# First loads of a four-layer transformer kernel moved between two DMA queues, and eight idle matmuls in place of ten

## The chip, the cores and the metric

The kernel runs on one core of a Trainium2 chip. The metric is the time of one execution on the device in microseconds (us); lower is better. Before the change it was 1632.44 us (median of three, 1632.38 to 1632.49).

## The reference

Two linear-attention layers (A) and two gated feed-forward layers (B) alternate on x of 2048 x 1024 in bf16. Only the start of the first layer A matters here: a layer norm of x, then the projection onto K.

```python
def _layernorm(x, axis=-1, eps=1e-5):
    m = jnp.mean(x, axis=axis, keepdims=True)
    v = jnp.var(x, axis=axis, keepdims=True)
    return (x - m) / jnp.sqrt(v + eps)
...
    x = x + _A_ref(_layernorm(x, axis=-1), A_wqkv, A_wo)   # q, k, v = x @ wqkv, ...
    x = x + _B_ref(_layernorm(x, axis=-1), B_W_gate, B_W_up, B_W_down)
    # and both once more
```

## The kernel before

The head loads x in blocks of 128 rows (256 KB; `load_x(t, c)` takes half c of block t) and the K weights k0 (in two halves of 512 KB) and k1 (1 MB). Everything without a queue goes to SyncE's queue. At the start of an execution TensorE's clock is slow: in the profile before, its matmuls start 0.43 us apart until 8.1 us and 0.22 us apart afterwards. So the head gives it matmuls on zeros ("idle" matmuls) while the first data come.

```python
def head(self):
    zero = self.ep.tile([P, NW], BF16, tag="e")
    nc.vector.memset(zero, 0.0)                      # after VectorE's other constants
    idle = self.ps3.tile([P, NW], F32, tag="b")
    for _ in range(10):
        nc.tensor.matmul(idle, lhsT=zero[:, 0:P], rhs=zero, start=True, stop=True)

    k0, k1, v0, q0, q1 = (ring.place() for _ in range(5))
    self.load_x(0, 0, nc.scalar)
    self.load_x(0, 1)
    self.load_x(1, None, nc.scalar)
    k0(0, H)
    self.load_x(2, None, nc.scalar)
    k0(H, 2 * H)
    self.load_x(3, None, nc.scalar)
    k1()
    q0()
    self.load_x(4)
    ...
```

The order of work for the first two blocks, which VectorE and ScalarE keep as written. Note `stat(1, 0)`, which stands before the scaling of block 0:

```python
def block0():
    stat(0, 0); stat(0, 1); rstd(0)      # VectorE, VectorE, ScalarE
    stat(1, 0)                           # first half of block 1
    scale(0, 0); scale(0, 1)             # VectorE
    t0 = turn(0, 0); t1 = turn(0, 1)     # TensorE: 4 transposes each
    t0("s"); stat(1, 1); rstd(1); t1("v")
    k(0, 0, between)                     # 8 matmuls; 1 to 4 read the first half of k0
```

`between` scales and transposes half of block 1 ahead of the last two of the eight. Then follow K unit (1,0) (block 1, k0), K unit (0,1) (block 0, k1), and so on.

## Time and profile before

| | |
|---|---|
| time, executions of the kernel before (31 timed in all, in four calls) | medians 1632.47 to 1632.53, all 1632.25 to 1633.73 us |
| the execution that was profiled | 1632.99 us, span 1631.2 us |

TensorE's busy time and its waits stand in the prediction below.

The timeline of VectorE in the profile before (start in us, duration in us, engine, line, operation, tiles; in brackets the idle time and what ended it):

```profile
3.61 1.29 DVE L142 BATCH_NORM_STATS2 st<-x 128x6 f32<-128x512 bf16 x2 [1.57 <-DMA x<-in_A_x_dram]
4.93 0.21 DVE L147 BATCH_NORM_AGGREGATE mv<-st 128x2 f32<-128x12 f32 x1
5.14 0.69 DVE L142 BATCH_NORM_STATS2 st<-x 128x6 f32<-128x512 bf16 x1
5.75 0.72 DVE L158 TENSOR_SCALAR x<-x,mv,rstd 128x512 bf16<-128x512 bf16 x2
```

TensorE's timeline in slices of 0.1 us shows where its clock became full (xN: so many in the slice, the first at the time in front):

```profile
8.06 0.62 PE L403 MATMUL ps<-t,xnT 128*128 128x512 bf16 x2
8.30 0.59 PE L403 MATMUL ps<-t,xnT 128*128 128x512 bf16 x2
8.52 0.38 PE L403 MATMUL ps<-t,xnT 128*128 128x512 bf16 x1
```

From 8.06 on the starts are 0.24 and 0.22 us apart, where they were 0.43 before.

### The profile page before, as it was taken

Reading aid. Unit: us, or ns where it says so; the run is one execution under the profiler, and the core shown is the slowest. Engines: PE = TensorE matmul, PEld = TensorE weight load, DVE = VectorE, ACT = ScalarE, POOL = GpSimd, SP = SyncE. Lnnn points to the kernel's source line nnn. Section 1 sums busy time; section 2 is a strip of 40 time slices with the busy share of each in tenths; the row PEclk is TensorE's granted clock in tenths of the full one; section 3 lists DMA queues with packets and bytes.
Section 4 is the critical chain, followed back from the end, with each engine's and each line's share of the span. In section 5 each row is a group of like instructions: output and inputs, shape, how many; then the busy total and the mean of one; then the engine's idle time right before and its main releaser. Section 6 shows DMA issues by size and latency. Waiting matters only on the chain.

```text
span 1631.2 us, 18462 instructions
## 1 busy us (share of the span) xinstructions
PE 1625.2 (100%) x7658; PEld 743.1 (46%) x7658; DVE 570.8 (35%) x947; ACT 331.2 (20%) x636; POOL 201.5 (12%) x134
## 2 busy tenths in 40 slices
PE   9999999999999999999999999999999999999999
PEld 4444444444444444444444444444444444444444
DVE  7855695113212222222264547941022111211211
ACT  6741212101110110111066312121011101101110
POOL 2349220000000000000023592100000000000000
PEclk9999999999999999999999999999999999999999
DMA  8313637448445445544550147464554454454452
GB/s 248 62 52 59 175 71 201 145 151 232 155 145 188 160 150 162 168 151 138 166 124 1 52 98 244 84 193 145 179 166 149 156 186 155 145 165 155 155 161 72
DMA packets 298245, 235.05 MB, mean 144 GB/s; under 512 B 101296, under 2 KB 294192, under 8 KB 298160
## 3 DMA queue, kind: packets, MB, share of 16 engines
q1 hardware_dynamic: 292832, 228.75, 47.5%
q10 hardware_dynamic: 5328, 5.11, 0.9%
q8 instruction: 60, 0.98, 0.2%
q14 instruction: 25, 0.20, 0.0%
HBM read 201.33 MB, written 8.39 MB: 129 GB/s over the span
## 4 chain that ended last, share of the span: by engine, by line
PE 98%; ACT 1%; DMA 0%; DVE 0%; issue 0%; SPq 0%
PE pu L628 24%; PE pg L628 24%; PE acc L652 23%; PE ps L403 12%; PE ps L520 7%; PE ps L437 7%; DMA t<-in_A_wqkv_dram 0%; PE kv L450 0%; PE fold L508 0%; PE acc_last L652 0%; ACT e L355 0%; ACT e L354 0%; ACT e L356 0%; PE tp L264 0%; DVE pq L362 0%
## 5 line engine op out<-in xcount | busy, mean ns | idle before, releaser
L628 PEld LDWEIGHTS <-t 128*128 128x128 bf16 x3584 | 350.7, 98 | 422.8
L628 PE MATMUL pu<-xnT,t 128*128 128x512 bf16 x1792 | 423.3, 379 | 0.0
L628 PE MATMUL pg<-xnT,t 128*128 128x512 bf16 x1792 | 423.3, 379 | 0.0
L652 PE MATMUL acc<-t,hT 128*128 128x512 bf16 x1764 | 382.5, 379 | 0.0
L634 DVE TENSOR_TENSOR hT<-pu,rg 128x512 bf16<-128x512 f32 x224 | 154.6, 690 | 572.9 <-PE pu L628 572.9
L633 ACT ACTIVATE rg<-pg 128x512 f32<-128x512 f32 x224 | 133.5, 596 | 737.4 <-PE pg L628 737.4
L652 PEld LDWEIGHTS <-hT 128*128 128x128 bf16 x1820 | 178.1, 98 | 209.0
L403 PE MATMUL ps<-t,xnT 128*128 128x512 bf16 x1024 | 224.7, 379 | 1.0 <-DMA t<-in_A_wqkv_dram 0.6
L403 PEld LDWEIGHTS <-xnT 128*128 128x128 bf16 x1024 | 99.8, 98 | 121.2 <-issue 1.8
L520 PE MATMUL ps<-T,pqT 128*128 128x512 bf16 x512 | 111.8, 379 | 0.0
L149 ACT ACTIVATE rstd<-mv,eps 128x1 f32<-128x1 f32 x64 | 18.7, 293 | 327.8 <-DVE mv L147 327.7
L669 DVE TENSOR_TENSOR xo<-x,acc 128x512 bf16<-128x512 f32 x31 | 21.3, 688 | 170.3 <-PE acc L652 170.3
L483 POOL TENSOR_TENSOR prod<-pq,zrow 128x1024 f32<-128x1024 bf16 x32 | 67.9, 2123 | 87.8 <-DVE den L488 75.6
L142 DVE BATCH_NORM_STATS2 stats<-x 128x6 f32<-128x512 f32 (+1 forms) x120 | 77.9, 672 | 0.8
L520 PEld LDWEIGHTS <-pqT 128*128 128x128 bf16 x512 | 50.1, 98 | 60.4
L417 POOL CAST ksum<-x 128x512 f32<-128x512 bf16 x2 | 1.7, 866 | 605.4 <-DVE x L362 605.4
L666 DVE TENSOR_TENSOR x<-x,acc 128x512 f32<-128x512 f32 x32 | 21.6, 674 | 138.5 <-PE acc L652 137.4
L419 POOL TENSOR_TENSOR ksum<-ksum,slab 128x512 f32<-128x512 f32 x46 | 53.6, 1171 | 86.3 <-DVE slab L362 76.8
L362 DVE SCALAR_TENSOR_TENSOR pq<-ps,e 128x512 bf16<-128x512 f32 x64 | 44.0, 688 | 55.7 <-ACT e L356 55.2
L495 POOL TENSOR_TENSOR pq<-pq,den 128x1024 bf16<-128x1024 bf16 x32 | 61.7, 1933 | 3.1 <-DVE den L490 3.1
L488 DVE TENSOR_REDUCE den<-prod 128x32 f32<-128x1024 f32 x32 | 38.9, 1217 | 52.6 <-POOL prod L483 52.6
L437 PE MATMUL ps<-slab,x 128*128 128x512 bf16 x256 | 56.6, 379 | 0.0
(58 smaller groups left out, 609.0 us busy)
## 6 DMA issues: line engine op xcount, KB each, us to landing
t<-in_B_W_gate_dram SPq DMA_DIRECT2D x56, 1024.0 KB, 7.0
t<-in_B_W_up_dram SPq DMA_DIRECT2D x56, 1024.0 KB, 5.4
t<-in_B_W_down_dram SPq DMA_DIRECT2D x64, 896.0 KB, 5.0
t<-in_A_wqkv_dram SPq DMA_DIRECT2D x11, 1024.0 KB, 6.2
t<-in_A_wo_dram SPq DMA_DIRECT2D x4, 1024.0 KB, 6.8
away<-x SPq DMA_DIRECT2D x8, 512.0 KB, 4.1
x<-away SPq DMA_DIRECT2D x8, 512.0 KB, 7.8
out_dram<-xo ACTq DMA_DIRECT2D x31, 128.0 KB, 2.3
```

The costliest lines, as they stand in the source:

```text
L142: self.nc.vector.bn_stats(out=stats[:, c, :], in_=src[:, c * fmax:(c + 1) * fmax])
L362: nc.vector.scalar_tensor_tensor(out=out, in0=ps, scalar=0.0, in1=e, op0=ALU.max, op1=ALU.add)
L403: nc.tensor.matmul(ps, lhsT=self.xnT[l, l_q][:, kt, j * P:(j + 1) * P], rhs=w[:, kt, :], start=(kt == 0), stop=(kt == KT - 1))
L419: nc.gpsimd.tensor_tensor(out=ksum[:, cols], in0=ksum[:, cols], in1=pk, op=ALU.add)
L437: nc.tensor.matmul(ps, lhsT=self.xn[l, t][:, d * P:(d + 1) * P], rhs=self.pk[l, t][:, h * NW:(h + 1) * NW], start=(t == 0), stop=(t == sel ...
L483: nc.gpsimd.tensor_tensor(out=prod, in0=pq_of[sc, j], in1=zrow, op=ALU.mult)
L495: nc.gpsimd.tensor_tensor(out=heads(pq), in0=heads(pq), in1=den[:, :].unsqueeze(2).to_broadcast([P, D // HD, HD]), op=ALU.mult)
L520: nc.tensor.matmul(ps, lhsT=pqT[sc][:, g, j * P:(j + 1) * P], rhs=T[g // 2][:, g % 2, n2 * NW:(n2 + 1) * NW], start=(g == 0), stop=(g == G ...
L628: nc.tensor.matmul(ps, lhsT=w[:, kt, fi * P:(fi + 1) * P], rhs=self.xnT[l, q][:, kt, :], start=(kt == 0), stop=(kt == KT - 1))
L633: nc.scalar.activation(out=rg, in_=pg, func=ACT.Relu)
L634: nc.vector.tensor_tensor(out=h[:, fi, :], in0=pu, in1=rg, op=ALU.mult)
L652: nc.tensor.matmul(ps[:, 0:n], lhsT=hT[ft // 4][:, ft % 4, j * P:(j + 1) * P], rhs=wd[:, k, i * n:(i + 1) * n], start=(ft == 0), stop=(ft ...
```

## The change

The intent: fewer bytes in front of the second half of k0, which TensorE waits for. Blocks 2 and 3 of x go behind the first weights on SyncE's queue, the halves of block 0 swap queues, and two idle matmuls are saved.

```diff
-        for _ in range(10):
+        for _ in range(8):
             nc.tensor.matmul(idle, lhsT=zero[:, 0:P], rhs=zero, start=True, stop=True)
 ...
-        self.load_x(0, 0, nc.scalar)
-        self.load_x(0, 1)
+        self.load_x(0, 0)
+        self.load_x(0, 1, nc.scalar)
+        k0(0, H)
         self.load_x(1, None, nc.scalar)
-        k0(0, H)
-        self.load_x(2, None, nc.scalar)
         k0(H, 2 * H)
-        self.load_x(3, None, nc.scalar)
+        self.load_x(2)
         k1()
+        self.load_x(3)
         q0()
```

## The prediction

> **What bounds the kernel now.** I read the page first (busy shares, chain that ended last), then the waits of TensorE over the whole span, then the chain and the timeline of the first 13 us, and last the transfers, one issue at a time.
>
> ```profile
> span 1631.2 us, 18462 instructions
> PE 1625.2 (100%) x7658; PEld 743.1 (46%) x7658; DVE 570.8 (35%) x947; ACT 331.2 (20%) x636; POOL 201.5 (12%) x134
> ```
>
> TensorE is busy for all but 6.0 us of the span. What the change can remove can only be among those 6 us, or in matmuls that run slowly. The view of TensorE's waits says which they are:
>
> ```profile
> PE idle L224 <- DVE zero L221: 2.1, 1, 2.1
> PE ps L403 <- DMA t<-in_A_wqkv_dram: 0.6, 1, 0.6
> PE ps L403 <- ACT xnT L271: 0.3, 1, 0.3
> ```
>
> Of the remaining 3.0 us, 2.9 lie after the last matmul (VectorE's last add ends at 1628.7, the rest is the output's landing). So after 9.48 us TensorE never waits, and whatever moves the matmul that starts there moves the end by as much. The chain of the first 30 us names what holds that matmul:
>
> ```profile
> 1.66 7.78 DMA t<-in_A_wqkv_dram
> 9.44 0.04 issue
> 9.48 0.59 PE ps L403 x2
> ```
>
> This is the second half of the first K weights (issued at 1.66, landed at 9.44; called k0b here, its first half k0a, the next K weights k1). TensorE's timeline up to that point:
>
> ```profile
> 2.10 4.45 PE L224 MATMUL idle<-zero 128*128 128x512 bf16 x10 [2.10 <-DVE zero L221]
> 6.34 1.06 PE L264 MATMUL tp<-ident,x 128*128 128x128 bf16 x8
> 7.66 1.24 PE L403 MATMUL ps<-t,xnT 128*128 128x512 bf16 x4 [0.26 <-ACT xnT L271]
> 9.48 0.38 PE L403 MATMUL ps<-t,xnT 128*128 128x512 bf16 x1 [0.58 <-DMA t<-in_A_wqkv_dram]
> ```
>
> The reader is to see that four K matmuls need only k0a and the fifth waits. Looked at in slices of 0.1 us, the idle matmuls start every 0.427 us (2.10, 2.50, 2.92 ... 5.91), the first K matmuls at 7.66, 8.06, 8.30, 8.52: the spacing falls from 0.40 to about 0.22 us near 8.1, where the clock becomes full. It stayed slow for 6.0 us after the first idle matmul.
>
> The transfers up to the landing of k0b, from a window that ends at 9.44:
>
> ```profile
> q1 hardware_dynamic: 1727, 1.72, 56.0%
> q10 hardware_dynamic: 576, 0.92, 26.8%
> ```
>
> q1 is SyncE's queue, q10 ScalarE's (packets, MB). ScalarE's 0.92 MB (half of x block 0, blocks 1, 2, 3) have all passed before k0b landed. Single issues, in us from issue to landing: k0a 1.19 + 4.6 = 5.8; x1 about 1.2 + 3.9 = 5.1; x2 1.67 + 6.2 = 7.9; x3 about 2.2 + 6.8 = 9.0; k1 about 2.2 + 10.2 = 12.4.
>
> **What the Trainium skill says.** "DMA: Bandwidth & Descriptors", section "Issuing engines are not separate DMA queues": transfers of ScalarE and SyncE share the same 16 engines and interleave; a second queue saves only issue time. The trace agrees: the total is 0.18 MB per 0.5 us both while q10 is active and when q1 is alone (345 to 385 GB/s). Same page, "Queues, rings and completion order": each engine takes turns between the queues, and completion is not in order of issue. The trace agrees: q1 had moved 1.72 MB when k0b landed, of which its own order needs only 1.18 (0.13 + 0.52 + 0.52), so 0.54 MB of k1 overtook it or was already under way. "TensorE: Matmul & The Clock Gate", "What's actually happening": the clock is halved until a free-running window of about 3.4 us has been busy. The trace shows the halved spacing and the step, but 6.0 us after the start rather than 3.4; with such a window ending at 8.1, the one before it (1.3 to 4.7) held 2.6 us of matmuls, 76%, and did not suffice. Same page, "Part 4: PE-mode transpose": transposes do not count as busy in the same way. No view of before tells.
>
> **The change, part by part.**
>
> *Queue of x blocks 2 and 3.* They leave q10, 0.52 MB, and stand on q1 behind k0b (x2) and behind k1 (x3). Bytes in front of k0b's landing: before 1.72 + 0.92 = 2.64 MB; after 1.72 + 0.39 = 2.11 MB, if the same overhang of 0.54 MB is kept. At 0.365 MB per us the difference is 0.53 / 0.365 = 1.45 us: k0b at about 8.0 in place of 9.44.
>
> *Halves of x block 0 swapped between the queues.* Both were issued at 0.74 to 0.76 and took 2.7 and 2.8 us; swapped, the first statistics may start at 3.48 in place of 3.61. But VectorE's order puts the first statistics of x1 (landed 5.07, begun 5.14) before the scaling of x0, so only some 0.05 us remain of 0.13.
>
> *Two idle matmuls fewer.* They took 2 x 0.427 us; the last starts at 5.08 in place of 5.91 and streams to about 5.5. The tenth held the array until 5.91 + 0.43 = 6.34, exactly where the first transpose begins, whose weights were loaded at 6.20. Without it the transposes begin at about 6.25, and through ScalarE's copy (0.60) the K matmuls at about 7.56 rather than 7.66.
>
> *With a full clock from then on.* Matmuls 1 to 4 end their issue at 7.56 + 4 x 0.217 = 8.43, later than k0b's 8.0, so the wait is gone. The fifth starts at 8.43 in place of 9.48: 1.05 us gained. The next limit is k1: before, K unit (0,1) starts at 10.81 + 8 x 0.217 = 12.55, with k1 there at 12.4, hardly any slack. After, k1 has x2 in front of it on q1 but not x2 and x3 on q10: 0.26 MB less, 0.7 us earlier, 11.6 to 11.7. So 0.9 of the 1.05 us can be kept. x2 (about 8.6) is needed by VectorE at about 10.3; x3 (about 12.3) at 14.23 - 0.9 = 13.3; both fit. The later weights have the same bytes ahead of them as before and are needed much later (q0 lands at 15.5 and is used after 24). Sum with a full clock: 1632.4 - 0.9 = **1631.5 us**.
>
> **The rivals.**
>
> *Late clock.* With eight, idle matmuls cover 2.10 to 5.5, 3.4 us, then a hole of 0.7 us to the first transpose, the transposes, another hole of 0.4 us. With ten there was no first hole. For it speaks that 76% of a window was not enough in the profile: a window over the new holes would hold about 1.1 idle us in 3.4, 68%, and would fail too, and the next one ends 3.4 us later, between 9.5 and 11.8. Against it: windows that end before about 6.1 see little of the hole (a third of the phases with a demand of 85%), and with a demand just over 76% three quarters pass. If late, matmuls from 7.56 take 0.427 us; the fifth starts at 9.27, k0b has long been there, only 0.2 us is won, and then each us of slow clock loses 0.49. Full clock at 9.5 means 0.1 us gained, at 10.5 +0.4, at 11.8 +1.0: about **1632.3 to 1633.4 us**, possibly different from run to run.
>
> *A weight or x block takes the wait over.* The estimate of k0b's landing rests on an unchanged overhang of 0.54 MB; k1 now shares the engines with fewer others and x2 sits on q1 next to it. Should k1 land no earlier than 12.4, K unit (0,1) can't start before, and the gain is only 12.55 - 12.45 = 0.1 us: about **1632.3**. For it: k1 is issued at the same place of an already filled queue. Against: fewer bytes in front, at a full rate throughout.
>
> *Hidden anyway.* If transposes or x0 are later rather than earlier (x0's second half behind ScalarE's own start), the first K matmuls shift by the same, but there is 1.05 us of room before the fifth would be later than now. I give this little weight.
>
> **Range and chances.** A full clock in time has about 55%: 1631.3 to 1631.8. A late clock or k1's wait, 45%: 1632.2 to 1633.4, centre 1632.8. The weighted mean is 0.55 x 1631.5 + 0.45 x 1632.8 = 1632.1; I say 1632.0, as the first is the denser. The range, 1631.2 to 1633.2, leaves out the latest clock. A change of 2% is 32 us; the head up to 9.48 us has nowhere near that, and nothing behind it is touched, so within 2% is all but certain (0.99).
>
> **What would show it.** Right: the wait of TensorE for the first K weights is gone or under 0.1 us, k0b lands near 8.0 and k1 near 11.7, transposes start near 6.25, the K matmuls near 7.56 follow each other at 0.22 us, and the fifth starts near 8.4. The late clock shows as K matmuls or transposes still spaced 0.43 and 0.107 us after 8 us; k1 as a wait of TensorE at K unit (0,1). Wrong altogether would be a new wait of TensorE after 13 us, or an end that moves by other than the shift of TensorE at 15 us.

## The result

The changed kernel took 1633.33 us (median of four: 1633.46, 1633.20, 1633.58 and 1631.89), the kernel before 1632.47 (median of four). The ratio is 1.0004, 95% interval 0.9986 to 1.0021: the same, within 2%. (A ratio is the mean time of one kernel's runs over that of the other's of the same rounds, so not quite the ratio of the medians.) The spread of 1.7 us is the changed kernel's.

TensorE's waits in the profile after (an execution of 1633.46 us):

```profile
PE idle L224 <- DVE zero L221: 2.1, 1, 2.1
PE tp L264 <- DVE x L158: 0.8, 1, 0.8
PE ps L403 <- ACT xnT L271: 0.3, 1, 0.3
```

The wait for k0 is gone; a wait of 0.8 us ahead of the first transposes is new. That is the hole that the two saved matmuls leave (block 1 of x, below, widens it). The transfers, from issue to landing, in windows around single issues (second half of k0, issued at 1.66, and k1, issued at 2.75), then the bytes moved by 7.78:

```profile
t<-in_A_wqkv_dram SPq DMA_DIRECT2D x1, 512.0 KB, 6.1
...
t<-in_A_wqkv_dram SPq DMA_DIRECT2D x1, 1024.0 KB, 8.7
...
q1 hardware_dynamic: 1511, 1.61, 65.0%
q10 hardware_dynamic: 288, 0.39, 13.7%
```

The second half of k0 is there at 7.8 in place of 9.44, k1 at 11.45 in place of 12.4, with 2.00 MB moved in place of 2.64. The transfers do what was meant. TensorE's timeline in slices tells where it went:

```profile
5.06 0.63 PE L224 MATMUL idle<-zero 128*128 128x512 bf16 x1
6.47 0.29 PE L264 MATMUL tp<-ident,x 128*128 128x128 bf16 x1 [0.78 <-DVE x L158]
...
8.16 0.64 PE L403 MATMUL ps<-t,xnT 128*128 128x512 bf16 x1
8.59 0.64 PE L403 MATMUL ps<-t,xnT 128*128 128x512 bf16 x1
9.02 0.64 PE L403 MATMUL ps<-t,xnT 128*128 128x512 bf16 x1
9.44 0.63 PE L403 MATMUL ps<-t,xnT 128*128 128x512 bf16 x1
9.87 0.58 PE L403 MATMUL ps<-t,xnT 128*128 128x512 bf16 x1
```

The K matmuls start at 7.77 and stand 0.43 us apart until after 10 us, although their weights have landed. The clock is still slow. K unit (1,0) starts at 11.20 (before: 10.81), as the last lines of the two timelines of 0 to 13 us show, first before, then after:

```profile
10.81 2.55 PE L403 MATMUL ps<-t,xnT 128*128 128x512 bf16 x11
11.20 2.12 PE L403 MATMUL ps<-t,xnT 128*128 128x512 bf16 x9
```

The span is 1631.6 (before: 1631.2). The difference of span and that start is 1620.40 here and 1620.39 before: the whole result is made in the first 11 us.

One more thing is new. VectorE's timeline after:

```profile
5.40 0.69 DVE L142 BATCH_NORM_STATS2 st<-x 128x6 f32<-128x512 bf16 x1 [0.28 <-DMA x<-in_A_x_dram]
6.01 0.72 DVE L158 TENSOR_SCALAR x<-x,mv,rstd 128x512 bf16<-128x512 bf16 x2
```

Block 1 landed at 5.4 (5.1 before), VectorE waited for it, and the scaling of block 0 was held by that.

### The profile page after: what moved, and what is told of

It reads as the page before. It is cut to its first block, busy times and chain, and to the rows that moved or that the text cites. A ratio compares the mean times of both kernels' runs of the same rounds, so it can differ in the third digit from the quotient of the medians.

```text
span 1631.6 us, 18458 instructions
## 1 busy us (share of the span) xinstructions
PE 1625.4 (100%) x7656; PEld 742.2 (45%) x7656; DVE 570.9 (35%) x947; ACT 331.3 (20%) x636; POOL 201.5 (12%) x134
## 4 chain that ended last, share of the span: by engine, by line
PE 98%; ACT 1%; DMA 0%; DVE 0%; issue 0%
PE pu L628 24%; PE pg L628 24%; PE acc L652 23%; PE ps L403 13%; PE ps L437 7%; PE ps L520 7%; PE kv L450 0%; PE fold L508 0%; PE acc_last L652 0%; ACT e L355 0%; DMA x<-in_A_x_dram 0%; ACT e L354 0%; ACT e L356 0%; PE tp L264 0%; DVE pq L362 0%
```

## The experiments

Twelve runs were made, each profiled and timed in five executions. The medians of before were 1632.53, 1632.53 and 1632.50 us. The theory: what the transfers gain is real, but with a hole after 3.4 us of idle matmuls the clock becomes full too late in some executions. The rivals: the new order of transfers costs by itself; or the number of matmuls decides and not the hole.

| run | queues | idle matmuls | times, us | median |
|---|---|---|---|---|
| changed_again | new | 8 | 1634.08, 1631.85, 1632.27, 1632.01, 1631.83 | 1632.01 |
| changed_third | new | 8 | 1632.05, 1633.85, 1632.08, 1632.26, 1632.08 | 1632.08 |
| new_queues_ten | new | 10 | 1632.07, 1631.91, 1632.03, 1632.17, 1632.39 | 1632.07 |
| new_queues_early_twelve | new | 12 from 1.2 us | 1632.10, 1632.15, 1632.02, 1632.11, 1632.15 | 1632.11 |
| early_twelve_again | new | 12 from 1.2 us | 1632.11, 1631.87, 1632.00, 1632.51, 1632.05 | 1632.05 |
| eight_late_start | new | 8 from 3.0 us | 1632.70, 1632.24, 1632.81, 1632.82, 1632.01 | 1632.70 |
| new_queues_none | new | 0 | 1633.51, 1633.15, 1634.27, 1633.14, 1633.84 | 1633.51 |
| old_queues_eight | old | 8 | 1633.15, 1634.46, 1632.33, 1632.49, 1632.38 | 1632.49 |
| old_queues_early_twelve | old | 12 from 1.2 us | 1632.85, 1633.57, 1632.68, 1632.31, 1632.95 | 1632.85 |
| third_on_scalar_ten | new, x2 on ScalarE's | 10 | 1632.43, 1632.47, 1632.24, 1632.14, 1631.91 | 1632.24 |
| early_eleven_halves | new, x1 in halves | 11 from 1.2 us | 1632.93, 1632.90, 1632.72, 1633.26, 1633.31 | 1632.93 |
| early_eleven_x1_first | x1 ahead of k0 | 11 from 1.2 us | 1632.70, 1632.42, 1632.26, 1631.83, 1632.29 | 1632.29 |

The first time of each row is the profiled execution. All are "the same" within 2%, with intervals some 0.1 to 0.15% wide on either side; what tells them apart is the groups of single times and the traces.

**The changed kernel again, twice.** No edit.

> The changed kernel once more, for the spread of its times (it had 1633.46, 1633.20, 1633.58 and 1631.89 us). Late clock (theory): the time follows when TensorE's clock becomes full, which differs from execution to execution; the five times spread over more than 1 us between about 1631.7 and 1633.7, while the kernel before stays within 0.2 us. Rival (the 1631.89 was a chance of the chip, the new order of transfers is what costs): times within 0.3 us around 1633.4. The profile's time should agree with the spacing of the K matmuls in it: about 1633.4 if they run at 0.43 us until after 10 us, about 1631.8 if at 0.22 us from the start.

> The changed kernel on one more chip, for the count of late executions (so far 4 of 9 at 1633.2 us or above, 5 at 1631.8 to 1632.3, none between). Late clock: both groups again, none between 1632.6 and 1633.0. Rival: one group.

With the first four there are 14 executions: nine from 1631.83 to 1632.27 (median 1632.05), five from 1633.20 to 1634.08 (median 1633.58), none between. Three of them were profiled, and these name the groups. The one of changed_third (1632.05 us), its TensorE timeline:

```profile
6.57 0.72 PE L264 MATMUL tp<-ident,x 128*128 128x128 bf16 x8 [1.04 <-DVE x L158]
7.66 1.47 PE L403 MATMUL ps<-t,xnT 128*128 128x512 bf16 x6 [0.36 <-ACT xnT L271]
...
9.87 3.41 PE L403 MATMUL ps<-t,xnT 128*128 128x512 bf16 x15
```

and the one of changed_again (1634.08 us):

```profile
7.01 1.03 PE L264 MATMUL tp<-ident,x 128*128 128x128 bf16 x8 [1.32 <-DVE x L158]
8.30 2.74 PE L403 MATMUL ps<-t,xnT 128*128 128x512 bf16 x6 [0.26 <-ACT xnT L271]
```

The same six K matmuls took 1.47 us with the full clock and 2.74 with the slow one. The same kernel does both. What differs most is when the clock became full: by the trace's record of the granted clock at 5.25 us in the first, while the idle matmuls still ran, and at 11.1 in the second. It is not all: in the second both halves of block 0 also landed later (at 4.1 and 4.3 us, against 3.3 and 3.5), so that its transposes start 0.44 us later for a reason that has nothing to do with the clock. In the profile after (1633.46 us) block 0 landed at 3.6 and 3.75, and the clock became full at 10.3. That the other eleven executions divide in the same way is inferred from their times.

**Ten idle matmuls.** The change's queues alone.

```diff
-        for _ in range(8):
+        for _ in range(10):
```

> The change's queues with ten idle matmuls. Late clock: there is no hole of 0.8 us before the transposes, the clock is full by about 8.2 us at the latest, the first K weights no longer gate; 1631.6 to 1632.0 us, spread under 0.5 us, about 0.7 under the kernel before. Rival (the order of the transfers costs, the idle matmuls do not matter): about 1633.3 us, as the changed kernel.

Five times from 1631.91 to 1632.39: no slow group, faster than before by 0.46 us in the median; the median lies just above the range that was expected. Its TensorE timeline shows no hole and no wait for weights:

```profile
6.38 1.04 PE L264 MATMUL tp<-ident,x 128*128 128x128 bf16 x8
7.68 1.47 PE L403 MATMUL ps<-t,xnT 128*128 128x512 bf16 x6 [0.26 <-ACT xnT L271]
```

The rival, that the order of the transfers costs, falls.

**Eight idle matmuls in the old order.** The kernel before with `range(8)`.

> The old queues with eight idle matmuls. Late clock: the hole is there (0.6 to 0.7 us), the clock is late in most executions; the times spread by more than 1 us, 1632.4 where it is in time (the second half of the first K weights still lands at 9.4) and up to 1633.6 where it is late. Rival (idle matmuls do not matter): 1632.4 us and narrow, as the kernel before.

One execution in five at 1634.46, 2 us above its others; three at 1632.33 to 1632.49. That a late group comes with eight in the old order too is not shown by this: the one execution has no trace, and it is the only one with a granted clock of 0.999, where all others, the late ones of the changed kernel included, have 1.000, so it may have lost its time in another way. Two of the 31 executions of the kernel before, with ten, also lie high (1633.31 and 1633.73), without a trace. That most executions would be late, as was expected, is wrong. The profiled one (1633.15) is not late by the clock, which was full at 5.1 us, still ahead of the hole: its transposes took 0.72 us in all, but it waited for the second half of k0 and for k1, 1.3 us in two waits.

**None, and eight without a hole.** For none the loop is taken out. For the other the zeros are written twice, at double width, so that the matmuls start later:

```diff
-        zero = self.ep.tile([P, NW], BF16, tag="e")
-        nc.vector.memset(zero, 0.0)
+        zero = self.ep.tile([P, 2 * NW], BF16, tag="e")
+        for _ in range(2):
+            nc.vector.memset(zero, 0.0)
```

> The change's queues with no idle matmul at all: the dose of the late clock. Late clock: no execution has a full clock at the first K matmul (7.7 us); [...]it becomes full between 9.3 and 12.8, and each us of K matmuls at half rate loses 0.49: no time at 1632.0 any more, all five between 1632.8 and 1634.5 us. Rival (the late executions have another cause, idle matmuls do nothing): the same two groups as with eight, some at 1631.9.

> Hole or number? The changed kernel with eight idle matmuls that start some 0.8 us later (their zeros are written twice, over twice the width), so that they run from about 2.9 to 6.3 us and no hole is left before the transposes. If the hole decides: the clock is full by 8.9 us at the latest (the longest that was seen from first matmul to full clock without a hole is 6.0 us), at most 0.6 us is lost: 1631.9 to 1632.5 us in all five, as with ten. If the number of idle matmuls (3.4 us of them) decides: two groups as in the changed kernel, some at 1633.2 us and above.

With none every execution is late (1633.14 to 1634.27), as expected. With eight that end at the transposes there is no late group: 1632.01 to 1632.82. The upper end is 0.3 us above what was expected. TensorE's timelines, first none, then eight without a hole:

```profile
7.63 2.74 PE L402 MATMUL ps<-t,xnT 128*128 128x512 bf16 x6 [0.26 <-ACT xnT L270]
```

```profile
3.02 3.59 PE L225 MATMUL idle<-zero 128*128 128x512 bf16 x8 [3.02 <-DVE zero L222]
6.41 1.06 PE L265 MATMUL tp<-ident,x 128*128 128x128 bf16 x8
7.73 1.96 PE L404 MATMUL ps<-t,xnT 128*128 128x512 bf16 x6 [0.26 <-ACT xnT L272]
```

The K matmuls took 1.96 us: in slices, the first two are 0.43 us apart, from 8.87 on 0.22. The clock was full 5.7 us after the first idle matmul, late enough to cost 0.6 us, but not the whole 1.3 of a hole. The same number of idle matmuls, no hole, no late group: this speaks for the hole and against the number. With the 5 of 14 of the changed kernel, five executions without a late one have a chance of some 11% (9/14 to the fifth power), so the rival is made unlikely, not ruled out. (The start was moved too; a hole alone, at the old start, could not be filled without more matmuls, which is the run with ten.)

**Earlier zeros.** The zeros are written first of all on VectorE, twelve matmuls run from 1.19 us; with the new queues (twice) and with the old ones.

```diff
+        self.zero = self.ep.tile([P, NW], BF16, tag="e")   # before the other constants
+        nc.vector.memset(self.zero, 0.0)
 ...
-        for _ in range(8):
+        for _ in range(12):
```

> The change's queues; the zeros that the idle matmuls read are written first of all on VectorE, so that twelve of them run from about 1.2 to 6.3 us. Late clock: with one more us of matmuls and no hole the clock is full before the first K matmul at about 7.7 in every execution; 1631.5 to 1631.8 us, spread under 0.2 us, faster than the kernel before by 0.7 to 0.9. Rival: 1633.3 us, as the changed kernel.

> The early twelve on the same chip as these, once more: 1632.0 to 1632.2 us in every execution; the kernel before at 1632.3 to 1632.8.

> The old queues with the zeros first and twelve idle matmuls: the clock part by itself without the transfers' part. If the second half of the first K weights holds TensorE in the old order (landing near 9 us), an earlier clock buys nothing: 1632.4 us, as the kernel before, narrow. If the gain of the early twelve came from the clock alone: 1632.1 us as with the new queues.

With the new queues: 1631.87 to 1632.51 in ten executions, the medians 1632.11 and 1632.05, no late one. That is 0.42 and 0.45 us under the kernel before, half of what was expected of it, and no better than ten idle matmuls at the old start (1632.07). The spread was 0.13 us in the first call, but 0.64 in the second. With the old queues the earlier clock buys nothing; the median (1632.85) is even 0.3 above the kernel before. Its TensorE timeline shows why nothing is gained:

```profile
7.41 1.04 PE L404 MATMUL ps<-t,xnT 128*128 128x512 bf16 x4 [0.37 <-ACT xnT L272]
9.32 0.59 PE L404 MATMUL ps<-t,xnT 128*128 128x512 bf16 x2 [0.88 <-DMA t<-in_A_wqkv_dram]
```

TensorE reaches its fifth K matmul earlier and waits 0.88 us for the second half of k0, which lands at 9.28. Why the median is above that of the kernel before stays open. So the queues' part gains, and only where the clock is in time.

**Block 2 on ScalarE's queue.**

```diff
-        self.load_x(2)
+        self.load_x(2, None, nc.scalar)
```

> Ten idle matmuls, the change's queues but for x block 2, which stays on ScalarE's queue. 0.26 MB more pass before the second half of the first K weights: by the bytes in front it lands some 0.7 us later than with the new queues (7.8), at about 8.5, where the fifth K matmul is due at about 8.5: 1632.1 to 1632.3 us. Block 1 of x landed 0.3 us later with nothing behind it on that queue (5.2 to 5.4 against 5.1); if that comes from the empty queue, it is back near 5.1 here, with no wait of VectorE for it. If the wait remains it is not the queue's filling.

The second half of k0 landed at 1.66 + 7.2 = 8.9, and TensorE waited for it:

```profile
8.90 0.59 PE L403 MATMUL ps<-t,xnT 128*128 128x512 bf16 x2 [0.45 <-DMA t<-in_A_wqkv_dram]
```

The time is between, 1632.24. A landing at 8.5 had been expected, 0.7 us after 7.8. On this chip the run without idle matmuls, with the new queues, had it at 1.66 + 6.6 = 8.3, and the one with block 1 in halves at 7.8, so that the 0.26 MB cost 0.6 to 1.1 us here; their bytes say 0.7. Over all profiles with the new queues it landed between 7.4 and 8.3. Block 1 still landed at 5.2 and VectorE still waited 0.24 us, so the idea that it came later because nothing stood behind it falls. From issue it took 3.9 us in the profile before, 4.0 and 4.1 in the two other profiles with the old queues, and with the new ones 4.0 to 4.3, in changed_again 4.7. The two overlap, so that it is not even shown that the queues delay it.

**Two tries at block 1.** Since VectorE waits for it, first in halves, then on SyncE's queue ahead of k0, both with zeros first and eleven idle matmuls.

```diff
-        self.load_x(1, None, nc.scalar)
+        self.load_x(1, 0, nc.scalar)       # early_eleven_halves
+        self.load_x(1, 1, nc.scalar)
```

```diff
+        self.load_x(1)                     # early_eleven_x1_first
         k0(0, H)
-        self.load_x(1, None, nc.scalar)
```

> A try at a version that beats both: new queues, zeros first, eleven idle matmuls (to about 5.9 us), and x block 1 in two halves, so that its first statistics (before the scaling of block 0 in VectorE's order) need only 128 KB. First half there at about 4.5 us, no wait of VectorE, transposes at about 6.0 in place of 6.3 to 6.5, K matmuls from about 7.3 at 0.22 us; the next limit is the second K weights at 11.4. 1631.8 to 1632.0 us, narrow, about 0.5 to 0.6 under the kernel before. If the wait for block 1 costs nothing: 1632.1 as the early twelve.

> A second try at a version that beats both: zeros first, eleven idle matmuls, x block 1 whole on SyncE's queue ahead of the first K weights (halves of it behind each other came too late). Block 1 at about 4.5 us in place of 5.2, transposes at about 6.0, K matmuls from 7.1; the second K weights at about 11.4 hold K unit (0,1), due at 11.0, so that only 0.1 to 0.2 us of it can be kept: 1631.9 to 1632.1 us, narrow. If x block 1 ahead delays the second half of the first K weights beyond 8.2, no gain over the early twelve (1632.1).

Both missed. In halves, the first half was in time (VectorE's wait is gone), but the second landed only at 7.8. The chain of waits of that run:

```profile
1.67 6.12 DMA x<-in_A_x_dram
7.79 0.02 issue
7.81 0.70 DVE st L144
```

The statistics that need it stand in VectorE's order ahead of the copy of transposed x, so TensorE waited 0.9 us for VectorE: 1632.93. With block 1 ahead, it landed at 4.3, but the weights paid, as the view of TensorE's waits shows (total, times, longest):

```profile
PE ps L404 <- DMA t<-in_A_wqkv_dram: 1.5, 3, 0.6
```

The first half of k0, its second half and k1 were each late by about half a microsecond; 1632.29, 0.2 behind the early twelve of the same chip.

## Why the prediction was right or wrong

*Same within 2%* was right, and needed no more than the 9.5 us of the head.

*The transfers.* Right. The second half of k0 at 7.8 in the profile after (said 8.0), k1 at 11.45 (11.6 to 11.7), 2.00 MB in front (2.11). The wait is gone in every profile with the change's queues as they are.

*The late clock.* The rival was right as a mechanism: two groups from execution to execution, the K matmuls still 0.43 us apart after 8 us, and ten idle matmuls end it; with the same eight without a hole none of five was late. Its share was given with the wait for k1 as 45%; it was 5 of 14. The wait for k1 itself did not come.

The prediction's reasoning with windows of 3.4 us, a length that it takes from the Trainium skill ("TensorE: Matmul & The Clock Gate", "What's actually happening"), can be redone as an estimate on all 14 profiles: go back in steps of 3.4 us from the moment at which the clock became full, and add up how long TensorE streamed in each window. With the transposes counted, the windows that ended in a full clock were filled to 87% or more, and all earlier ones to 78% or less. In the profile after, the window with the hole (3.47 to 6.87) was filled to 72% and the next one to 87%; in changed_third a window ended at 5.25 us, ahead of the hole, filled to 93%. So it depends on where the windows fall whether the hole does harm. Without the transposes the sum does not come out: in the profile before, 62% (4.71 to 8.11) would have been enough where 78% (1.31 to 4.71) had not been. So by this estimate transposes count here, against the sentence on them that the prediction cites ("Part 4: PE-mode transpose"); the prediction said that no view of before tells, but these two windows of it do.

*The levels.* Both were too low: in time 1631.5 was said and 1632.05 measured, 0.5 us more; late 1632.3 to 1633.4 was said and 1633.20 to 1634.08 measured, 0.7 to 0.9 more. So the first median of four, three of them late, fell 0.1 us above the range of 1631.2 to 1633.2; the median of all 14 (1632.17) is inside it. The step that failed is "Sum with a full clock: 1632.4 - 0.9". The 0.9 was read from a profile, and it holds against that profile: its execution took 1632.99 us, and with the full clock the K unit (1,0) starts at 9.87 in place of 10.81, 0.94 earlier, with 1632.05 us. But it was taken off the median of the timed executions, which were 0.5 us faster than the profiled one. In those the head must have been shorter by as much: their spans are 1630.5 to 1630.7 for times near 1632.4, and in all kernels where nothing waits later the span is 1620.4 us plus the start of K unit (1,0), which puts it near 10.2 rather than 10.8. The second half of k0 must have landed by about 8.9 there in place of 9.44, since from the fifth K matmul to K unit (1,0) it takes 1.33 us even with a full clock; why it did, no trace of such an execution shows. The typical gain to be had was thus 0.45 us, not 0.9. The late level has the same 0.5 us in it; the rest is of the size of the later transposes (see the two idle matmuls below).

*The size of the late clock.* "Each us of slow clock loses 0.49" was right: in the profile after, the clock was slow from 7.77 to about 10.3, which makes 1.2 us; against changed_third the stretch from the first K matmul to K unit (1,0) was 3.43 in place of 2.21 us.

*Two idle matmuls fewer, transposes at 6.25.* Wrong by 0.2 to 0.3 us: they start at 6.47 (6.57 in changed_third; 7.01 in changed_again, where block 0 was late too), since block 1 landed at 5.4 to 5.5 and its statistics stand in front of the scaling. The prediction saw that order, but put the landing before at 5.07; it was 5.12, and VectorE began at 5.14, so there was no slack for a later landing. The 0.13 us from the swapped halves of block 0 did not come either: the first statistics began at 3.59 in the profile after, against 3.61 before (3.31 and 4.14 in the other two). Saving the two matmuls won nothing at all; the tenth had only just held the transposes.

Over all, the nine executions in time are 0.45 us under the kernel before and the five late ones 1.1 us above it; the mean of the 14 is 1632.6 us, that of the 31 executions before 1632.6 as well. The gain of the queues is spent on the hole of the clock.

## What to carry to other kernels

A gain read from one profile must be taken off the time of that same execution; with gains under 0.1%, time the execution that was profiled and look at several others before adding or subtracting. Filler matmuls that wake the clock should run into the real work without a hole: with the new queues, 5 of 14 executions with the hole were late, and none of the 25 with ten or twelve, or with eight up to the transposes. Starting them earlier brought nothing more (medians 1632.05 and 1632.11 against 1632.07). After a transfer has been taken out of the way, count who else was hidden behind the wait: here the slow clock and the next block of x.

## What the Trainium skill lacked or had wrong

- "TensorE: Matmul & The Clock Gate" says that the step to the full clock comes around 4 us into sustained matmuls, give or take 0.5, and in its table at the end to keep TensorE busy for 4 us. Where no hole came before it, it came between about 3.0 us (old_queues_eight: first idle matmul at 2.10, full at 5.1) and 6.0 us (the kernel before: 2.10, 8.1) after the first idle matmul. With a hole of 0.8 to 1.3 us after 3.4 us of matmuls it came after 8.2 and 9.0 us in two profiles. Its remark that the window runs freely and the cold count differs from run to run agrees with the two groups.
- The sentence of the same page on transposes, which the prediction cites, does not fit: counted as busy they make sense of all 14 profiles, left out they do not (62% enough where 78% was not; see "The late clock" above, an estimate).
- The same page warns of idle gaps over about 3 us; it does not say what a shorter hole does while the clock is still slow. Here, with one of 0.8 to 1.3 us, 5 of 14 executions came out about 1.5 us longer than the others (medians 1633.58 and 1632.05); in the two of them that were profiled the late clock makes up most of it.
- "DMA: Bandwidth & Descriptors" says that the engines take turns between queues packet by packet, and that a second queue saves only issue time. It does not say how bytes divide. Between 4.0 and 4.5 us before, ScalarE's queue (rows of 2 KB) moved 0.13 MB in 67 packets and SyncE's (runs of 1 KB) 0.07 MB in 69: equal turns by the profile's packets, so twice the bytes for the queue with the longer rows.
